# Interleaving VectorE's passes of neighbouring steps in the first block of a dense-GELU forward and backward kernel, and holding two early weight loads behind ScalarE's first activation

## The chip, the cores and the metric

The kernel runs on one core of one Trainium2 chip. The metric is the device time of one execution in microseconds; a time shown is the median of several runs. The engines are named as the profile names them: PE (TensorE), DVE (VectorE), ACT (ScalarE), POOL (GpSimd) and SP (SyncE, which here only issues transfers).

## The reference

A dense layer with GELU and a second dense layer, and the gradients of everything for a given `grad_out`. All tensors are bf16; S = 2048 rows, D = 448, F = 1792.

```python
def _fwd_reference(x, w1, b1, w2, b2):
    h = jnp.einsum("bsd,df->bsf", x, w1) + b1
    h = _gelu(h)                      # the tanh form
    return jnp.einsum("bsf,fd->bsd", h, w2) + b2

def reference(x, w1, b1, w2, b2, grad_out):
    _out, _vjp = jax.vjp(_f, x, w1, b1, w2, b2)   # _f is _fwd_reference
    _grads = _vjp(grad_out)
    return (_out, *_grads)            # out, gx, gw1, gb1, gw2, gb2
```

With u = x w1 + b1, h = gelu(u), q = grad_out w2^T and gh = q * gelu'(u), the outputs are out = h w2 + b2, gx = gh w1^T, gw1 = x^T gh, gb1 = the column sums of gh, gw2 = h^T grad_out and gb2 = the column sums of grad_out.

## The kernel before

**Tiling.** The rows are cut into four blocks of 512 (`NB`, `SB`), the hidden features into seven pairs of tiles of 128 (`NPAIR`), taken in the order `FP = [1, 2, 3, 4, 5, 6, 0]`. One *step* is one pair in one block, so there are 28 steps (`NSTEP`). Everything is held transposed, features on the partitions: for a step PE makes u (2 x 512 columns in two PSUM banks, `pu`) and q (two banks, `pq`), and ACT and DVE make h (`hT`) and gh (`ghT`) from them in SBUF. Blocks that are done feed the `o` units (out) and `x` units (gx), whose matmuls (`ps`) are put between those of u and q. After the steps come the weight gradients (lines 666 to 781), 180.7 us into the profile.

**One step on ACT and DVE.** In the first eight steps (`NSINGLE = 8`) each step is done by itself; from step 8 on two steps share an instruction. `copy_u` (L346, L348) adds the bias and brings u from PSUM to `U4`. `act_square` (L355) makes a = c u^2 and `act_gelu` (L352) makes h. `dve_cubic` makes z = (a + const) u in two passes (L359 *cubic*, L360 *cubic\*u*), and `act_tanh` (L364) takes the tanh of z in place. `dve_gate` then has four passes: L370 *slope* (a + const, times -2), L371 *slope\*h* (times h), L372 *both* (one pass over a and z together, 128x2048), L373 *gate* (z times a). `dve_gh` (L386) makes gh = (1 - z) q, reading q from PSUM. The tiles a and z of a step lie in `AZ`, which has three places, step k in place k mod 3; `U4` has two places.

**The order of the work.** It is written out by hand (`tc.manual_schedule()`): each engine runs its instructions in the order of the calls, and waits on semaphores for what it needs. In the loop over i (lines 519 to 563) PE makes u of step f = i + 2 and q of step i, with matmuls of the o and x units between them. ACT has the Tanh of step i, the two copies of u of step f, Gelu of f, then Square of f. DVE has cubic of step i + 1, the four passes of gate i, then gh i (in step 1 gate first). q has one pair of PSUM banks in these steps (`two_banks(0)`, L252), so q of step i can be started (`q_tail`, through `pe_tail_pair`) when gh of step i - 1 has read the banks. u of steps 0 and 2 to 9 has one pair of banks as well, so the u products of step f wait for the copies of step f - 1.

**The start.** SP and ACT issue the first transfers. ACT's queue has the columns 256 to 512 of w1 (`load_w1`) and their last 64 rows (`load_rest`), then the warm-up activation, which brings the table load with it, and then the columns 512 to 768 of w1 and the rest of `wt1`. ACT's sequencer issues the load of columns 512 to 768 while the table load runs, since nothing makes it wait. SP has x of the first block in two transposed halves of 256 rows (L150, L153), then w1's columns 768 to 1024 and further loads. Ten matmuls on zeros (`NWAKE`) run on PE until the data is there. Step 0's u is made in the two halves of x (`pe_u_fulls`, L239).

`behind(eng, transfer)` (L126) puts a no-op on an engine that waits until the given instruction, or the given transfer, is done. What stands behind it in the queue of that engine waits as well.

Of the kernel before, what the change touches and what calls it, by code (L numbers as in the profile page):

```python
# [19 lines left out]
def kernel(  # L20
# [15 lines left out]
    nc = tc.nc  # L36
# [88 lines left out]

    def behind(eng, transfer):  # L126
        tc.add_manual_dep(eng.nop().ins, transfer.ins.name, mybir.DependencyInfo(mybir.DependencyClass.Sync, mybir.DependencyReason.DATA),
                          reason="small loads behind those needed first")

    def load_w2(eng, t0, t1):  # L130
        return eng.dma_start(out=w2_sb[:, t0:t1, :], in_=w2[t0 * P:t1 * P, :].rearrange("(ft p) d -> p ft d", p=P))
# [20 lines left out]
    load_rest(nc.scalar, 256, 512)  # L152
    nc.sync.dma_start_transpose(out=xT[0][:, :, halves[1]], in_=wide(x2, ROW0[0] + SB // 2, SB // 2, 0))  # L153
    warm = stg.tile([P, 1], F32, name="warm", tag="warm", bufs=1)
    nc.scalar.activation(out=warm[:], in_=zero[:, 0:1], func=ACT.Gelu_apprx_tanh)
    load_w1(nc.scalar, 512, 768)
    load_rest(nc.scalar, 512, 1024)
    load_w1(nc.sync, 768, 1024)
# [46 lines left out]
    def place(first, ks):  # L205
        return AZ[:, first:first + 2 * len(ks), :]

    def part_a(ks):
        k = ks[0]
        return place(4 * (k % 3) if k < NSINGLE else SETS[k // 2 % 2] + 2 * (k % 2), ks)  # L210

    def part_z(ks):
        k = ks[0]
        return place(4 * (k % 3) + 2 if k < NSINGLE else 2 * (k % 2), ks)
# [10 lines left out]
    def rows(store, ks):  # L225
        b = ks[0] // NPAIR
        return store[b][:, 2 * (ks[0] % NPAIR):2 * (ks[-1] % NPAIR) + 2, :]
# [122 lines left out]
    def act_gelu(fs):  # L350
        for r in runs(fs):
            nc.scalar.activation(out=rows(hT, r), in_=part_u(r), func=ACT.Gelu_apprx_tanh)  # L352

    def act_square(ks):
        nc.scalar.activation(out=part_a(ks), in_=part_u(ks), func=ACT.Square, scale=math.sqrt(3.0 * GELU_A * GELU_C))  # L355

    def dve_cubic(ks):
        z = part_z(ks)
        nc.vector.tensor_scalar(out=z, in0=part_a(ks), scalar1=3.0 * GELU_C, scalar2=None, op0=ALU.add)  # L359
        nc.vector.tensor_tensor(out=z, in0=z, in1=part_u(ks), op=ALU.mult)  # L360

    def act_tanh(ks):
        z = part_z(ks)
        nc.scalar.activation(out=z, in_=z, func=ACT.Tanh, scale=-1.0 / 3.0)  # L364

    def dve_gate(ks, between=None):
        a_, z_ = part_a(ks), part_z(ks)
        if ks[0] < NSINGLE:
            both = place(4 * (ks[0] % 3), ks + ks)
            nc.vector.tensor_scalar(out=a_, in0=a_, scalar1=GELU_C, scalar2=-2.0, op0=ALU.add, op1=ALU.mult)  # L370
            nc.vector.tensor_tensor(out=a_, in0=a_, in1=rows(hT, ks), op=ALU.mult)  # L371
            nc.vector.tensor_scalar(out=both, in0=both, scalar1=1.0, scalar2=math.sqrt(0.5), op0=ALU.add, op1=ALU.mult)  # L372
            nc.vector.tensor_tensor(out=z_, in0=z_, in1=a_, op=ALU.mult)  # L373
            return
        nc.vector.tensor_scalar(out=a_, in0=a_, scalar1=GELU_C, scalar2=None, op0=ALU.add)
        for r in runs(ks):
            nc.vector.tensor_tensor(out=part_a(r), in0=part_a(r), in1=rows(hT, r), op=ALU.mult)
        nc.vector.tensor_scalar(out=a_, in0=a_, scalar1=-0.5, scalar2=None, op0=ALU.add)
        if between is not None:
            between()  # L380
        nc.vector.tensor_scalar(out=z_, in0=z_, scalar1=1.0, scalar2=None, op0=ALU.add)
        nc.vector.tensor_tensor(out=z_, in0=z_, in1=a_, op=ALU.mult)

    def dve_gh(k):
        single = k < NSINGLE
        nc.vector.scalar_tensor_tensor(out=rows(ghT, [k]), in0=part_z([k]), scalar=1.0, in1=PQ[k][:],  # L386
                                       op0=ALU.subtract if single else ALU.add, op1=ALU.mult, reverse0=single)
# [73 lines left out]
    def evictions(most=NS):  # L461
        for un in finished[:most]:
            un.evict()
        del finished[:most]
# [23 lines left out]
    copy_u(0, "av")  # L488
    act_square([0])
    act_gelu([0])  # L490
    dve_cubic([0])
    pe_u_fulls(1)
    pe_tails([1], [])
    copy_u(1, "av")
# [14 lines left out]
    side_by_side(q_of(0, 0), q_of(0, 1))  # L509
    units_side(uns[0], False, tiles(1))  # L510
    side_by_side(q_of(0, 1, True), q_of(0, 0, True))
    dve_gate([0])
    dve_cubic([1])
    dve_gh(0)
    copy_u(2, "aa")
    act_tanh([1])
    act_gelu([2])
    act_square([2])
    for i in range(1, NSINGLE):
        f = i + LEAD  # L520
        if i < 6:
            between = [(uns[1], False, tiles(i)), (uns[0], True, tiles(i)[:1]), (uns[0], True, tiles(i)[1:]), (uns[1], True, tiles(i))]
        elif i == 6:
            between = [(uns[0], True, tiles(i)), (uns[1], False, tiles(i)[:1]), (uns[1], False, tiles(i)[1:]), (uns[1], True, tiles(i))]
        else:
            between = [(uns[0], False, range(6, 10)), (uns[0], False, range(10, 12)), (uns[0], False, range(12, 14)), (uns[0], True, range(0, 6))]
        open_u(f)
        open_q(i)
        side_by_side(u_of(f, 0, True), u_of(f, 1, True))
        units_side(*between[0])  # L530
        side_by_side(u_of(f, 1), u_of(f, 0))
        units_side(*between[1])
        pe_tail_pair(f, i, 1)
        pe_tail_pair(f, i, 0)
        units_side(*between[2])
        side_by_side(q_of(i, 0), q_of(i, 1))
        units_side(*between[3])
        side_by_side(q_of(i, 1, True), q_of(i, 0, True))
        if i < 6:
            units_side(uns[0], False, tiles(i + 1))  # L540
        if i > 1:
            act_tanh([i])
        evictions(2)
        copy_u(f, "aa")
        evictions()
        act_gelu([f])
        act_square([f])
        if i == 1:
            dve_gate([i])
            dve_cubic([i + 1])  # L550
        else:
            dve_cubic([i + 1])
            dve_gate([i])
        dve_gh(i)
        if i == 6:
            open_two(1, 2)
            uns = [open_units[-2:]]
            units_side(uns[0], False, range(0, 6))
        if i == 7:
            units_side(uns[0], True, range(6, NF))  # L560
        traffic(i)
        if i >= 6:
            stores(2, f - 1)
# [20 lines left out]
    for n in range(nq):  # L584
        i = NSINGLE + n
        k = NSINGLE + 2 * n
        ks = [k, k + 1]
        fs = [k + 2, k + 3] if k + 2 < NSTEP else []
        nxt = [k + 4, k + 5] if n >= 2 and k + 4 < NSTEP else []
        if n == 0:  # L590
            dve_cubic([k + 1])
            evictions()
        act_tanh(ks)
        dve_gate(ks, evictions)
        if n <= 2:
            for f in fs:
                pe_u_fulls(f)
        if n < 2:
            pe_tails(fs, ks)
            for q in ks:  # L600
                pe_q_fulls(q)
            for f in fs:
                copy_u(f, "aa")
            for q in ks:
                dve_gh(q)
            open_one()
            pieces(28, k + 1, k - 1)
            act_square(fs)
            act_gelu(fs)
            evictions(1)  # L610
            dve_cubic(fs)
        else:
            if fs:
                pe_tails(fs[::-1], ks[::-1])
            for f in fs[::-1]:
                copy_u(f, "aa")
            pe_q_rows(ks, nxt)
            for q in ks[::-1]:
                dve_gh(q)
            if nxt:  # L620
                open_u(nxt[0])
                side_by_side(u_of(nxt[0], 0, True), u_of(nxt[0], 1, True), slice(0, 1))
                open_two(1, 2)
                uns = open_units[-2:]
                units_side(uns, False)
                side_by_side(u_of(nxt[0], 0, True), u_of(nxt[0], 1, True), slice(1, None))
                units_side(uns, True)
                side_by_side(u_of(nxt[1], 1), u_of(nxt[1], 0))
                side_by_side(u_of(nxt[0], 1), u_of(nxt[0], 0))
            elif fs:  # L630
                uns, held = two_units(order_a[2:4]), two_units(order_a[0:2])
                units_side(uns, False)
                units_side(held, False)
                pe_tails([], [k + 2, k + 3])
                units_side(uns, True)
            if fs:
                act_square(fs)
                act_gelu(fs)
                dve_cubic(fs)
        if i == 8:  # L640
            nc.gpsimd.dma_start(out=g_low[0:DL, :], in_=gT[1][DL:P, 0, :])
            g_swap[1] = g_low
        if i == 15:
            nc.gpsimd.dma_start(out=g_low[DL:P, :], in_=gT[3][0:DL, 0, :])
            g_swap[3] = g_low
        traffic(i)
        stores(3, k + 1)
# [164 lines left out]
```

## Time and profile before

| what | value |
|---|---|
| median of 3 runs | 270.99 us (270.85 to 271.34) |
| the profiled execution | 270.91 us, its span 269.1 us |
| busy: PE, DVE, ACT, POOL | 262.2, 175.8, 138.7, 40.5 us |
| PE's first product of u, first and second half of x | 5.94 and 7.21 us |
| start of step 8's work on PE | 53.2 us |
| start of the weight gradients on PE | 180.7 us |
| granted TensorE clock | full speed in the whole span |

The time of an execution is the span in the profile plus what lies around it, here 1.8 us. A line of the view in order of time has the start in us from the start of the span, the duration, the engine, the line of the kernel and the operation, out<-in, the shapes and a count; what ended the engine's idle time ahead of it stands in brackets. A line of the chain of waits has a start, a length and what the end of the kernel depended on in that stretch. A line of the view of waits has who waited for whom, the total in us, how often, and the longest. A queue's line has packets, MB, and the time that its packets took as a share of the 16 DMA engines' time; q1 is SP's queue and q10 ACT's.

### The profile page before, as it was taken

What the parts mean: (1) busy time and instruction counts of PE and PEld (TensorE: products, weight loads), DVE (VectorE), ACT (ScalarE), POOL (GpSimd) and SP (SyncE); (2) the same over time, 40 slices, a digit from 0 to 9 for tenths busy, and PEclk for the clock granted to TensorE, in tenths of its full rate; (3) what the DMA queues carried; (4) which work ended last, traced back from release to release, by engine and by line L of the source; (5) the groups of instructions that cost most, each with busy time, mean ns of one, the idle gap of its engine ahead of it and who ended that gap; (6) DMA issues with size and microseconds to landing.
All of it is one profiled execution on the core that took longest, in us unless ns stands there. A gap on an engine that the chain in (4) does not pass through costs nothing.

```text
span 269.1 us, 4993 instructions
## 1 busy us (share of the span) xinstructions
PE 262.2 (97%) x2082; PEld 157.3 (58%) x2082; DVE 175.8 (65%) x202; ACT 138.7 (52%) x162; POOL 40.5 (15%) x52
## 2 busy tenths in 40 slices
PE   6999999999999999999999999999999999999995
PEld 2358567844445665555657888874444665555554
DVE  2599999899999889687898831219999991000000
ACT  2699889799995867968668420022111211121111
POOL 1001004011002020110202030311600008900000
PEclk9999999999999999999999999999999999999999
DMA  7999999999999996172561449999411102998971
GB/s 159 249 259 190 181 154 228 171 251 211 274 232 227 253 217 156 37 189 53 152 148 47 78 86 258 357 216 263 106 40 39 51 20 50 213 227 211 163 160 34
DMA packets 111734, 44.46 MB, mean 165 GB/s; under 512 B 91040, under 2 KB 110576, under 8 KB 111712
## 3 DMA queue, kind: packets, MB, share of 16 engines
q1 hardware_dynamic: 104608, 36.14, 66.1%
q0 software_dynamic: 1856, 4.30, 5.7%
q10 hardware_dynamic: 5248, 3.71, 5.1%
q8 instruction: 16, 0.26, 0.4%
q14 instruction: 6, 0.05, 0.1%
HBM read 7.23 MB, written 14.23 MB: 80 GB/s over the span
## 4 chain that ended last, share of the span: by engine, by line
PE 85%; DVE 8%; ACT 3%; DMA 2%; SPq 0%; issue 0%; DVEq 0%; ACTq 0%
PE ps L263 27%; PE ps_v L764 16%; PE ps_w L732 14%; PE pq L263 11%; PE pu L263 9%; PE pu L242 3%; PE ps_w L743 2%; PE pq L303 2%; PE ps L416 2%; DMA xT<-in_x_dram 2%; DVE ghT L386 1%; DVE AZ L360 1%; ACT AZ L355 1%; DVE AZ L372 1%; DVE AZ L371 1%; DVE AZ L373 1%
## 5 line engine op out<-in xcount | busy, mean ns | idle before, releaser
L263 PE MATMUL ps<-w_sb,hT 64*128 64x448 bf16 x432 | 51.7, 349 | 0.3 <-ACT hT L352 0.3
L263 PE MATMUL pq<-gT,w2T 64*128 64x512 bf16 x338 | 50.0, 376 | 0.6 <-DVE ghT L386 0.4
L346 ACT ACTIVATE U<-pu,b1T 128x512 bf16<-128x512 f32 x54 | 33.3, 686 | 18.8 <-PE pu L263 18.8
L386 DVE SCALAR_TENSOR_TENSOR ghT<-AZ,pq 128x1024 bf16<-128x1024 bf16 x28 | 33.8, 1220 | 13.4 <-PE pq L263 12.1
L764 PE MATMUL ps_v<-g_nat,h_nat 128*128 128x448 bf16 (+1 forms) x240 | 42.6, 340 | 0.0
L263 PE MATMUL ps<-w1T_sb,ghT 64*128 64x448 bf16 x392 | 40.8, 349 | 0.0
L430 POOL DMA_DIRECT2D out_dram<-st x32 | 19.1, 601 | 138.8 <-ACT st L427 85.7
L263 PEld LDWEIGHTS <-hT 64*128 64x128 bf16 x432 | 28.9, 94 | 14.8 <-ACT hT L352 0.8
L732 PE MATMUL ps_w<-gh_nat,x_nat 128*128 128x512 bf16 (+1 forms) x192 | 36.5, 352 | 0.0
L764 PEld LDWEIGHTS <-h_nat 128*128 128x128 bf16 x240 | 23.3, 98 | 19.3 <-DMA out_dram<-st 0.3
L263 PEld LDWEIGHTS <-ghT 64*128 64x128 bf16 x392 | 28.6, 94 | 9.3
L263 PE MATMUL pu<-xT,w_f 64*128 64x512 bf16 x228 | 33.4, 376 | 0.0
L263 PEld LDWEIGHTS <-w2T 64*128 64x128 bf16 x344 | 25.7, 94 | 10.3 <-PE pq L263 0.4
L364 ACT ACTIVATE AZ<-AZ 128x2048 bf16<-128x2048 bf16 (+1 forms) x18 | 27.5, 1526 | 7.7 <-DVE AZ L360 7.6
L718 DVE TENSOR_TENSOR acc<-acc,gh_nat 128x1792 f32<-128x1792 f32 x14 | 30.0, 2142 | 0.5
L732 PEld LDWEIGHTS <-x_nat 128*128 128x128 bf16 x192 | 18.7, 98 | 17.9 <-issue 0.4
L355 ACT ACTIVATE AZ<-U 128x1024 bf16<-128x1024 bf16 (+1 forms) x19 | 27.6, 1454 | 0.7 <-DVE U L348 0.4
L352 ACT ACTIVATE hT<-U 128x1024 bf16<-128x1024 bf16 (+1 forms) x20 | 27.7, 1388 | 0.2
L767 ACT CAST st<-ps_v 128x448 bf16<-128x448 f32 (+1 forms) x15 | 7.6, 507 | 34.8 <-PE ps_v L764 32.3
L427 ACT CAST st<-ps 128x448 bf16<-128x448 f32 x20 | 9.8, 531 | 30.4 <-PE ps L263 29.0
L735 ACT CAST st<-ps_w 128x512 bf16<-128x512 f32 (+1 forms) x12 | 6.4, 532 | 28.0 <-PE ps_w L732 28.0
L263 PEld LDWEIGHTS <-w_f 64*128 64x128 bf16 x228 | 15.1, 94 | 8.5 <-issue 0.2
(58 smaller groups left out, 214.6 us busy)
## 6 DMA issues: line engine op xcount, KB each, us to landing
hT_dram<-hT SPq DMA_DIRECT2D x28, 256.0 KB, 3.1
out_dram<-st POOLq DMA_DIRECT2D x32, 112.0 KB, 3.8
x_nat<-in_x_dram SPq DMA_DIRECT2D x1, 1792.0 KB, 10.3
g_nat<-in_grad_out_dram SPq DMA_DIRECT2D x1, 1792.0 KB, 15.4
out_dram<-st ACTq DMA_DIRECT2D x13, 112.0 KB, 3.3
out_dram<-st ACTq DMA_DIRECT2D x9, 128.0 KB, 1.7
w_f<-in_w_dram SPq DMA_DIRECT2D x5, 192.0 KB, 4.6
w_sb<-in_w_dram SPq DMA_DIRECT2D x4, 224.0 KB, 3.9
```

The costliest lines, as they stand in the source:

```text
L242: nc.tensor.matmul(PU[f][a][:, rs], lhsT=w1_f[:, kt, cols(p, a)], rhs=xT[b][:, kt, rs], start=(kt == 0 and rs.start == 0), stop=False, ski ...
L263: mm = nc.tensor.matmul(ps, lhsT=w, rhs=m, start=start, stop=stop, tile_position=(hf.start, 0), skip_group_check=True)
L346: nc.scalar.activation(out=dst, in_=PU[f][a][:], func=ACT.Identity, bias=bias)
L352: nc.scalar.activation(out=rows(hT, r), in_=part_u(r), func=ACT.Gelu_apprx_tanh)
L355: nc.scalar.activation(out=part_a(ks), in_=part_u(ks), func=ACT.Square, scale=math.sqrt(3.0 * GELU_A * GELU_C))
L364: nc.scalar.activation(out=z, in_=z, func=ACT.Tanh, scale=-1.0 / 3.0)
L386: nc.vector.scalar_tensor_tensor(out=rows(ghT, [k]), in0=part_z([k]), scalar=1.0, in1=PQ[k][:], op0=ALU.subtract if single else ALU.add, o ...
L427: nc.scalar.copy(out=st[:, 0:D], in_=self.ps)
L430: nc.gpsimd.dma_start(out=(out2 if self.kind == "o" else gx2)[r:r + P, :], in_=st[:, 0:D])
L718: nc.vector.tensor_tensor(out=v, in0=in0, in1=gh_nat[:, b, :, j, :], op=ALU.add)
L732: nc.tensor.matmul(ps[:, 0:n * P], lhsT=x_nat[:, st_, kt * P:(kt + 1) * P], rhs=gh_nat[:, b, ft0:ft0 + n, j, :], start=(st_ == 0), stop=(s ...
L764: nc.tensor.matmul(ps[:, 0:w], lhsT=h_nat[ft][:, st_, :], rhs=g_nat[:, st_, h * w:(h + 1) * w], start=(st_ == 0), stop=(st_ == NS - 1))
```

## The change

Four things are edited.

1. DVE's passes in steps 0 to 7. They are called by name through a new function, `dve_chain`, in another order. A step has the same seven passes on the same tiles. In step i (2 to 6) the order is now both i, cubic\*u i+1, gate i, slope i+1, gh i, slope\*h i+1, cubic f. Steps 0, 1 and 7 are the run-in and the run-out of that, and cubic and cubic\*u of step 9 move into step 7.
2. ACT makes Square ahead of Gelu from step 2 on, in the loop and just before it.
3. The warm-up activation is given to `behind` on ACT, so ACT's queue waits until the activation is done before it issues the loads that stand behind it.
4. The branch of `dve_gate` for single steps goes away, since `dve_chain` has its passes.

```diff
-    nc.scalar.activation(out=warm[:], in_=zero[:, 0:1], func=ACT.Gelu_apprx_tanh)
+    behind(nc.scalar, nc.scalar.activation(out=warm[:], in_=zero[:, 0:1], func=ACT.Gelu_apprx_tanh))
     load_w1(nc.scalar, 512, 768)
     load_rest(nc.scalar, 512, 1024)
...
     def dve_gate(ks, between=None):
         a_, z_ = part_a(ks), part_z(ks)
-        if ks[0] < NSINGLE:
-            both = place(4 * (ks[0] % 3), ks + ks)
-            nc.vector.tensor_scalar(out=a_, in0=a_, scalar1=GELU_C, scalar2=-2.0, op0=ALU.add, op1=ALU.mult)
-            nc.vector.tensor_tensor(out=a_, in0=a_, in1=rows(hT, ks), op=ALU.mult)
-            nc.vector.tensor_scalar(out=both, in0=both, scalar1=1.0, scalar2=math.sqrt(0.5), op0=ALU.add, op1=ALU.mult)
-            nc.vector.tensor_tensor(out=z_, in0=z_, in1=a_, op=ALU.mult)
-            return
...
+    def dve_chain(*names):
+        for name in names:
+            op, k = name.split()
+            k = int(k)
+            a_, z_ = part_a([k]), part_z([k])
+            if op == "cubic":
+                nc.vector.tensor_scalar(out=z_, in0=a_, scalar1=3.0 * GELU_C, scalar2=None, op0=ALU.add)
+            elif op == "cubic*u":
+                nc.vector.tensor_tensor(out=z_, in0=z_, in1=part_u([k]), op=ALU.mult)
+            elif op == "slope":
+                nc.vector.tensor_scalar(out=a_, in0=a_, scalar1=GELU_C, scalar2=-2.0, op0=ALU.add, op1=ALU.mult)
+            elif op == "slope*h":
+                nc.vector.tensor_tensor(out=a_, in0=a_, in1=rows(hT, [k]), op=ALU.mult)
+            elif op == "both":
+                both = place(4 * (k % 3), [k, k])
+                nc.vector.tensor_scalar(out=both, in0=both, scalar1=1.0, scalar2=math.sqrt(0.5), op0=ALU.add, op1=ALU.mult)
+            elif op == "gate":
+                nc.vector.tensor_tensor(out=z_, in0=z_, in1=a_, op=ALU.mult)
+            else:
+                dve_gh(k)
...
-    dve_cubic([0])
+    dve_chain("cubic 0", "cubic*u 0")
...
-    dve_gate([0])
-    dve_cubic([1])
-    dve_gh(0)
+    dve_chain("slope 0", "slope*h 0", "both 0", "cubic 1", "gate 0", "cubic*u 1", "slope 1", "gh 0", "slope*h 1")
     copy_u(2, "aa")
     act_tanh([1])
+    act_square([2])
     act_gelu([2])
-    act_square([2])
...
         copy_u(f, "aa")
         evictions()
+        act_square([f])
         act_gelu([f])
-        act_square([f])
         if i == 1:
-            dve_gate([i])
-            dve_cubic([i + 1])
+            dve_chain("both 1", "cubic 2", "gate 1", "cubic*u 2", "slope 2", "gh 1", "slope*h 2", "cubic 3")
+        elif i < 7:
+            dve_chain(f"both {i}", f"cubic*u {i + 1}", f"gate {i}", f"slope {i + 1}", f"gh {i}", f"slope*h {i + 1}", f"cubic {f}")
         else:
-            dve_cubic([i + 1])
-            dve_gate([i])
-        dve_gh(i)
+            dve_chain("both 7", "cubic*u 8", "gate 7", "cubic 9", "gh 7", "cubic*u 9")
...
         if n == 0:
-            dve_cubic([k + 1])
             evictions()
```

More of the change, by code (lines that the diff above doesn't have):

```diff
@@ L127, in behind @@
         tc.add_manual_dep(eng.nop().ins, transfer.ins.name, mybir.DependencyInfo(mybir.DependencyClass.Sync, mybir.DependencyReason.DATA),
-                          reason="small loads behind those needed first")
+                          reason="loads behind what is needed first")
     def load_w2(eng, t0, t1):
```

## The prediction

> **What bounds the kernel now.** I read the page first: TensorE (PE) is the busy engine, and the rest of the page has nothing that could replace it. A step below is one index k, i or f of the code.
>
> ```profile
> span 269.1 us, 4993 instructions
> PE 262.2 (97%) x2082; PEld 157.3 (58%) x2082; DVE 175.8 (65%) x202; ACT 138.7 (52%) x162; POOL 40.5 (15%) x52
> ```
>
> PE's idle time is 6.9 us in all, so only a few us could be won without taking matmuls away, so the second view is what PE waited for:
>
> ```profile
> PE pu L242 <- DMA xT<-in_x_dram: 1.6, 2, 1.1
> PE pq L263 <- DVE ghT L386: 0.4, 2, 0.2
> ```
>
> The 0.4 us behind VectorE (DVE) is too small a figure. Matmuls overlap, so PE counts as busy for some 0.38 us after it stopped starting new ones. The third view, PE in order of time, shows starts: first a step that isn't held up (i = 2), then one that is (i = 4).
>
> ```profile
> 20.49 0.92 PE L263 MATMUL pu<-xT,w_f 64*128 64x512 bf16 x6
> ...
> 22.35 0.38 PE L263 MATMUL pu<-xT,wt 64*128 64x512 bf16 x1
> 22.46 0.38 PE L263 MATMUL pq<-gT,w2T 64*128 64x512 bf16 x1
> ...
> 29.93 0.96 PE L263 MATMUL pu<-xT,w_f 64*128 64x512 bf16 x6
> ...
> 31.79 0.38 PE L263 MATMUL pu<-xT,wt 64*128 64x512 bf16 x1
> 32.39 0.37 PE L263 MATMUL pq<-gT,w2T 64*128 64x512 bf16 x1 [0.22 <-DVE ghT L386]
> ```
>
> From the tail of u to the tail of q PE takes 0.11 us in step 2 and 0.60 in step 4. The same view has 0.52 in step 3 (26.89 to 27.41), 0.60 in step 5 (36.77 to 37.37) and 0.40 in step 6 (41.94 to 42.34), and nothing of the sort in step 7 or later. Less 0.11 each, that is 0.41 + 0.49 + 0.49 + 0.29 = 1.68 us. By the starts of the steps (20.49, 25.02, 29.93, 34.91, 39.89) an unhindered step takes 4.53 and the next three 4.91, 4.98 and 4.98: 0.38 + 0.45 + 0.45, and with step 6's 0.29 it is 1.57. I use 1.6.
>
> Why PE is held up is in the chain of waits, which runs through DVE from 23 to 37 us; this is one step of it:
>
> ```profile
> 31.11 1.22 DVE ghT L386
> 32.34 0.35 DVE AZ L359
> 32.70 0.69 DVE AZ L360
> 33.40 0.35 DVE AZ L370
> ...
> 36.09 1.23 DVE ghT L386
> 37.37 0.37 PE pq L263
> ```
>
> DVE is never idle and takes 36.09 - 31.11 = 4.98 us a step, 0.45 more than PE. The q banks are one buffer in these steps, so PE's q tail of step i waits for dve_gh(i - 1), and PE goes at DVE's pace until the longer work of steps 6 and 7 lets DVE catch up. From 42.34 on PE never waits for DVE again.
>
> **The change, part by part.**
>
> *New order on DVE.* The same seven operations a step, on the same shapes, by the rows of 25 to 40 us: 0.42 + 0.69 (cubic) + 0.42 + 0.69 (slope) + 0.69 (both) + 0.69 (gate) + 1.22 (gh) = 4.82. The old order has five places where an operation reads what the one ahead wrote; those start 0.03 to 0.11 after its end (in DVE's order of time L360 begins at 32.70 where L359 ended at 32.67; L372 at 34.57 after 34.46). Two neighbours are independent:
>
> ```profile
> 32.25 0.42 DVE L359 TENSOR_SCALAR AZ<-AZ 128x1024 bf16<-128x1024 bf16 x1
> 32.70 0.69 DVE L360 TENSOR_TENSOR AZ<-AZ,U 128x1024 bf16<-128x1024 bf16 x1
> 33.31 0.42 DVE L370 TENSOR_SCALAR AZ<-AZ 128x1024 bf16<-128x1024 bf16 x1
> ```
>
> L370 starts at 33.31 though L360 runs from 32.70 for 0.69, to 33.39; L359 starts at 32.25 though L386 runs to 32.33. So an independent neighbour starts 0.08 early. In the new order of steps 2 to 6 (both i, cubic*u i+1, gate i, slope i+1, gh i, slope*h i+1, cubic f) every input is at least two operations old. With 0.08 won at all seven the step is 4.82 - 0.56 = 4.26; with nothing won it is 4.82. I take the first: three of the new seven are kinds of neighbours seen to overlap in this trace (products followed by a one-input pass twice; and two one-input passes, L378 to L381 at 56.01 + 0.69 against 56.62), and these three alone give 4.58. DVE then needs less than PE's 4.53, and the 1.6 us go.
>
> The Trainium skill ("VectorE: DVE Perf Modes", section "The DRAIN you can't avoid") speaks against this: every VectorE operation is followed by a flush of the pipe, and eight copies took the same time with a semaphore after each as with one after the last. By that rule order would be free, DVE would stay at 4.98 and the sum would lose its 1.6 us. The starts at 33.31 and 32.25 above do not agree with it, so I go by the rows.
>
> *What is late next.* In a PE step of 4.53 counted from its first u product: the copies of u can start at about 2.5 and end at 3.75 (1.27); Square and Gelu follow to about 5.7 and the next step's Tanh to 6.65 (1.04 to 1.06 each, 0.1 overlapped). The next copies are due at 7.0, so ScalarE (ACT) has 0.35 spare; its busy time of 4.2 in a step says the same. Tanh's input, cubic*u, is ready before then, since it now stands second on DVE. DVE's both starts at 6.7, that is 2.15 in its own step; both, cubic*u, gate and slope take it to about 4.35; q's last product ends at 4.43 (24.92 against 20.49), gh runs from 4.5 to 5.7, and the next q tail is at 4.53 + 1.97 = 6.50 (22.46 against 20.49). PE has 0.8 us of cover.
>
> *Square ahead of Gelu on ACT, from f = 2.* No new work and no second table load (one in the trace). Gelu's output comes 0.95 later. Its first reader is the o product at 20.11; Gelu of step 2 ends at 18.11 before and at 19.06 then, cover 1 us. Later readers come a step after. Square comes 0.95 earlier, which the cubic at the end of DVE's step needs. Cost 0.
>
> *Earlier cubic 9 and the split around step 7.* One 0.42 operation ahead of gh 7, which waited 0.81 us for PE anyway. Cost 0.
>
> *The warm-up activation ahead of ACT's later loads.* The load of w1's columns 512 to 768 goes from an issue at 1.86 to just after 3.30 (3.10 + 0.20), 1.45 later; the load of wt behind it from 3.47 to about 3.9. ACT itself has nothing else until 8.38. The first load landed 4.4 us after its issue, so then at about 7.7; PE wants it at 8.49. wt would land at 7.9 (4.0 after issue) and is wanted at 9.90. SP's queue has no new wait; its loads share the DMA engines. What this gives back is in the DMA queues from 3.9 to 4.5 us:
>
> ```profile
> q10 hardware_dynamic: 197, 0.10, 81.1%
> q1 hardware_dynamic: 17, 0.00, 2.9%
> ```
>
> ACT's queue (q10) holds the engines while the second half of x (q1, issued from 2.12 to 3.40) hardly moves; it lands at 7.2 and PE starts on it at 7.21, after a wait of 0.46. Everything after depends on that start: copies at 8.38, the chain above, and the first products of u. From 3.7 to 5.9 q10 took 44.4% of 2.2 us, 0.98; some 0.84 of it is the moved load (384 of 448 rows). At best x comes 0.84 earlier. At worst all of it falls into the second half's own stretch, 4.5 to 6.5, where q10 took 23.5% of 2 us, 0.47, already: 0.98 - 0.47 = 0.5 later. A lower bound from another row: the transposed load of equal size issued at 8.46 landed 3.6 us after issue, against 5.1 here, which would be 1.5 earlier. I take 0.4 earlier, about the middle of -0.84 and +0.5 with a lean to the gain, because the moved load won't be on the engines much before 4.6 (the first ACT load was issued at 0.72, and from 1 to 2 us the queues moved only 8 GB/s), when part of the second half should be through.
>
> *The sum.* The profiled execution took 270.91 for a span of 269.1, 1.8 around it, and lies 0.08 under the median of 270.99. 270.91 - 1.6 - 0.4 = 268.9. No PE wait shows after 42.34, so what is won there is kept to the end unless a transfer is late: the nearest is gT of block 1, which lands at 45.2 and is wanted at 48.39, then at 46.4.
>
> **Rivals.**
> - *x doesn't come earlier.* The moved load meets the second half of x rather than the first; between 5.0 and 5.8 the queues moved only 117 GB/s, and if that comes from mixing transposed and plain loads it may come again. DVE's part stays: 270.91 - 1.6 + (0 to 0.5) = 269.3 to 269.8.
> - *Only part of the overlap.* If the four unseen kinds of neighbours (one ending in a product or in gh) win nothing and wait a little, the step stays between 4.6 and 4.82 and PE still waits 0.1 to 0.3 in four steps. 270.91 - 0.64 - 0.4 = 269.9 at 4.82.
> - *Order is free on DVE.* Step stays 4.98, only x's 0.4 is left: 270.5, or no change if x doesn't move.
> - *Slower: ACT becomes the pace.* In the new order DVE's last operation of a step, cubic f, waits for ACT's Square f, which stands behind both copies, and everything behind it on DVE waits too. If the loop copies, Square, cubic, both, cubic*u, Tanh, copies took over 4.98 a step, PE would wait longer than before. ACT's 4.2 a step must grow by 0.8 to get there. With 5.2 in five steps it is 5 x 0.22 = 1.1 more, less x's 0.4: 271.6. Against it: the schedule above has 0.35 spare in that loop.
>
> **How the numbers follow.** Forecast (both parts, x 0.1 to 0.84 earlier, 268.4 to 269.2): 0.45. x much earlier (to 1.5, 267.8): 0.07. x not earlier: 0.24. Part of the overlap: 0.10. Order free: 0.07. Slower: 0.07. About 0.2% (0.54 us) is what can be told from no change here. Faster by that: 0.45 + 0.07 + 0.24 + most of 0.10 = 0.85; within it: 0.08 (order free, and the edge of the others); slower: 0.07. The range leaves out order free, slower and the lowest cases: 268.1 to 270.1.
>
> **What the new profile will show.** DVE's operations start 0.08 before the end of the one ahead, its step follows PE at about 4.53, with a wait for q's product ahead of each gh. The intervals u tail to q tail are 0.11 in steps 3 to 6. PE's second start on x is near 6.8, and the u product of step 1 follows without a wait for w1. I am wrong if DVE's step stays above 4.6, if PE waits for ACT in steps 2 to 6, if x lands after 7.2, or if PE shows new waits after 46 us.

## The result and the profile after

The changed kernel takes 269.01 us (median of 6 executions, 268.56 to 269.56) beside 270.81 for the kernel before on the same chip (270.58 to 271.34): a ratio of 0.9933, 95% interval 0.9915 to 0.995. The prediction was 268.9, with a range of 268.1 to 270.1. The profiled execution took 268.56 with a span of 266.8, 2.3 shorter than the 269.1 of before.

The head and the chain of the page after:

```profile
span 266.8 us, 5001 instructions
PE 261.6 (98%) x2082; PEld 159.9 (60%) x2082; DVE 173.4 (65%) x202; ACT 138.7 (52%) x162; POOL 40.3 (15%) x52
PE 94%; ACT 2%; DMA 2%; DVE 0%; issue 0%; ACTq 0%
```

DVE has left the chain that sets the end. All of what PE still waits for (who waited for whom, total us, times, longest):

```profile
PE pw L188 <- DVE AZ L142: 1.2, 1, 1.2
PE pu L242 <- DMA xT<-in_x_dram: 0.4, 1, 0.4
PE ps L263 <- ACT hT L352: 0.3, 1, 0.3
```

The wait for gh is gone, and the one for x is 0.4 in place of 1.6. The first and last lines stand in the same view of before too. PE in order of time, first the start, then steps 4 and 5:

```profile
5.76 1.47 PE L242 MATMUL pu<-xT,w_f 128*128 128x256 bf16 x12 [0.39 <-DMA xT<-in_x_dram]
7.17 0.60 PE L263 MATMUL pu<-xT,wt 64*128 64x512 bf16 x2
7.70 1.47 PE L242 MATMUL pu<-xT,w_f 128*128 128x512 bf16 x6
...
28.76 0.91 PE L263 MATMUL pu<-xT,w_f 64*128 64x512 bf16 x6
...
30.63 0.38 PE L263 MATMUL pu<-xT,wt 64*128 64x512 bf16 x1
30.73 0.38 PE L263 MATMUL pq<-gT,w2T 64*128 64x512 bf16 x1
...
32.27 0.91 PE L263 MATMUL pq<-gT,w2T 64*128 64x512 bf16 x6
...
33.30 0.91 PE L263 MATMUL pu<-xT,w_f 64*128 64x512 bf16 x6
```

The twelve products of step 0 on the two halves of x now run without a break, and the next group starts at 7.70, where it started at 8.49 before: 0.79. In step 4 the tail of q follows the tail of u after 0.10 (0.60 before), and the step takes 33.30 - 28.76 = 4.54. Steps 3 to 6 give the 1.57 that they lost before. 0.79 + 1.57 = 2.36, against 2.3 between the spans.

DVE in order of time, from gh of step 3 to gh of step 4. L400 is gh, L389 slope\*h, L383 cubic, L392 both, L385 cubic\*u, L394 gate, L387 slope:

```profile
28.69 1.22 DVE L400 SCALAR_TENSOR_TENSOR ghT<-AZ,pq 128x1024 bf16<-128x1024 bf16 x1
29.83 0.68 DVE L389 TENSOR_TENSOR AZ<-AZ,hT 128x1024 bf16<-128x1024 bf16 x1
30.43 0.42 DVE L383 TENSOR_SCALAR AZ<-AZ 128x1024 bf16<-128x1024 bf16 x1
31.00 0.69 DVE L392 TENSOR_SCALAR AZ<-AZ 128x2048 bf16<-128x2048 bf16 x1 [0.15 <-ACT AZ L364]
31.61 0.69 DVE L385 TENSOR_TENSOR AZ<-AZ,U 128x1024 bf16<-128x1024 bf16 x1
32.21 0.68 DVE L394 TENSOR_TENSOR AZ<-AZ 128x1024 bf16<-128x1024 bf16 x1
32.82 0.42 DVE L387 TENSOR_SCALAR AZ<-AZ 128x1024 bf16<-128x1024 bf16 x1
33.23 1.22 DVE L400 SCALAR_TENSOR_TENSOR ghT<-AZ,pq 128x1024 bf16<-128x1024 bf16 x1
```

Add start and duration: five of the seven passes end 0.07 to 0.09 after the next one has started (28.69 + 1.22 = 29.91 against 29.83). DVE's step is 33.23 - 28.69 = 4.54, PE's pace, and DVE is held twice in it. *Both* waits 0.15 for ACT's Tanh. And gh starts only 0.01 ahead of the end of slope (32.82 + 0.42 = 33.24), 0.05 after q's last product of step 4 (32.27 + 0.91 = 33.18); that hold is too short for a bracket.

The DMA queues from 3.9 to 4.5 us (packets, MB, share of the engines' time):

```profile
q1 hardware_dynamic: 291, 0.07, 82.4%
q10 hardware_dynamic: 14, 0.00, 3.0%
```

Before it was the other way round, with 81.1% for ACT's q10. The halves of x land at 5.72 and 6.37 (5.90 and 7.17 before). The load of w1's columns 512 to 768 is issued at 3.33, lands at 7.46 and is read at 7.70.

### The profile page after: what moved, and what is told of

The parts are those of the page before. It is cut to its first block, busy times and chain, and to the rows that moved or that the text cites. A ratio compares the mean times of both kernels' runs of the same rounds, so it can differ in the third digit from the quotient of the medians.

```text
span 266.8 us, 5001 instructions
## 1 busy us (share of the span) xinstructions
PE 261.6 (98%) x2082; PEld 159.9 (60%) x2082; DVE 173.4 (65%) x202; ACT 138.7 (52%) x162; POOL 40.3 (15%) x52
## 4 chain that ended last, share of the span: by engine, by line
PE 94%; ACT 2%; DMA 2%; DVE 0%; issue 0%; ACTq 0%
PE ps L263 29%; PE ps_v L774 16%; PE ps_w L742 14%; PE pq L263 13%; PE pu L263 12%; PE pu L242 4%; PE ps_w L753 2%; PE pq L303 2%; PE ps L430 2%; DMA xT<-in_x_dram 2%; ACT AZ L355 1%; ACT hT L352 1%; DVE U L348 0%; ACT U L346 0%; ACT AZ L364 0%
## 5 line engine op out<-in xcount | busy, mean ns | idle before, releaser
L263 PE MATMUL ps<-w_sb,hT 64*128 64x448 bf16 x432 | 50.7, 349 | 0.3 <-ACT hT L352 0.3
L400 DVE SCALAR_TENSOR_TENSOR ghT<-AZ,pq 128x1024 bf16<-128x1024 bf16 x28 | 33.9, 1220 | 12.8 <-PE pq L263 11.8
L263 PEld LDWEIGHTS <-w2T 64*128 64x128 bf16 x344 | 26.3, 94 | 9.5 <-PE pq L263 0.4
```

Of the source, the lines that this page charges most:

```text
L263: mm = nc.tensor.matmul(ps, lhsT=w, rhs=m, start=start, stop=stop, tile_position=(hf.start, 0), skip_group_check=True)
```

## The experiments

The theory: parting the dependent passes shortens DVE's step by what overlaps (1.6 us), and holding ACT's loads brings the start forward (0.4 or more), each without the other. The rivals were the ones on record, above all that the order on DVE is free, that the exchange of Square and Gelu does part of the work, and that the moved load only shifts the wait to another transfer. Each run stands beside the kernel before on the same chip. The first three versions below and the first repeat of the change shared one chip (before: 270.73). The two more passes, Gelu ahead of Square, the second repeat and Gelu of step 1 first shared another (270.90). ACT's loads later still, the third repeat and the two versions with the stores held shared a third (270.75).

### The new order alone

The changed kernel without the wait on ACT:

```diff
-    behind(nc.scalar, nc.scalar.activation(out=warm[:], in_=zero[:, 0:1], func=ACT.Gelu_apprx_tanh))
+    nc.scalar.activation(out=warm[:], in_=zero[:, 0:1], func=ACT.Gelu_apprx_tanh)
```

> The new order on VectorE and Square ahead of Gelu, without the wait of the warm-up activation. Theory (the predicted sum, DVE's part): the step on DVE falls from 4.98 to what PE needs, 4.53, the starts from u tail to q tail are 0.11 in steps 3 to 6, x still lands near 7.2; about 1.6 us less than before, 0.994 of its time. Rival (order is free on DVE): step 4.98, no change. Rival (the whole gain is the earlier start): no change either.

269.26 us (269.19 to 269.51), ratio 0.9946 [0.9934, 0.9959]: 1.47 under the kernel before. The second half of x lands at 7.10 (7.17 before). Of PE's waits the one for x is still there (1.1, where it was 1.6), and there is none for DVE's gh:

```profile
PE pu L242 <- DMA xT<-in_x_dram: 1.1, 2, 0.7
```

The order brings its part without the start.

### The wait alone

The kernel before with `behind` on the warm-up activation:

```diff
-    nc.scalar.activation(out=warm[:], in_=zero[:, 0:1], func=ACT.Gelu_apprx_tanh)
+    behind(nc.scalar, nc.scalar.activation(out=warm[:], in_=zero[:, 0:1], func=ACT.Gelu_apprx_tanh))
```

> The kernel before with the warm-up activation's wait alone. Theory: the second half of x lands near 6.4 instead of 7.2, and all that follows, DVE's chain too, starts 0.8 earlier; PE still waits 1.6 us for gh. In the profile 0.8 us less than before; by the median anything from 0.2 to 0.8 less, since the runs of the changed kernel lie 1.0 us apart and those of before 0.8. Rival (the chain on DVE takes the earlier start back): same time as before.

269.77 us (269.67 to 270.32), ratio 0.9966 [0.9954, 0.9979]: 0.96 less than before, over twice the 0.4 of the prediction. PE at the start, in order of time:

```profile
5.50 1.47 PE L242 MATMUL pu<-xT,w_f 128*128 128x256 bf16 x12
6.90 0.60 PE L263 MATMUL pu<-xT,wt 64*128 64x512 bf16 x2
7.66 1.47 PE L242 MATMUL pu<-xT,w_f 128*128 128x512 bf16 x6 [0.16 <-DMA w_f<-in_w_dram]
...
16.75 0.38 PE L263 MATMUL pu<-xT,wt 64*128 64x512 bf16 x1
```

Here x came so early (second half landed at 6.06) that the moved load of w1 was late: it landed at 7.62, and PE waited 0.16. That wait cost nothing. The tail of u of step 1 starts at 16.75, 9.85 after that of step 0 (6.90); before, the two are 17.82 - 7.96 = 9.86 apart, with a wait of 0.27 for Gelu of step 1 between them that is gone here. So the 1.06 won at step 0's tail is still there at step 1's (17.82 - 16.75 = 1.07). PE's intervals for gh in steps 3 to 6 stay (0.52, 0.59, 0.60, 0.40).

### Two of five dependent pairs parted

The kernel before; in steps 2 to 7 only cubic\*u and slope change places, which parts two pairs and leaves three:

```diff
-            dve_cubic([i + 1])
-            dve_gate([i])
+            a_, z_, z2 = part_a([i]), part_z([i]), part_z([i + 1])
...
+            nc.vector.tensor_scalar(out=z2, in0=part_a([i + 1]), scalar1=3.0 * GELU_C, scalar2=None, op0=ALU.add)
+            nc.vector.tensor_scalar(out=a_, in0=a_, scalar1=GELU_C, scalar2=-2.0, op0=ALU.add, op1=ALU.mult)
+            nc.vector.tensor_tensor(out=z2, in0=z2, in1=part_u([i + 1]), op=ALU.mult)
+            nc.vector.tensor_tensor(out=a_, in0=a_, in1=rows(hT, [i]), op=ALU.mult)
...
```

> The kernel before, and in steps 2 to 7 only cubic*u and slope exchanged on DVE, so that two of the five neighbours that read the output of the one ahead are parted; Tanh's input comes about 0.3 later than before, and nothing else moves. Theory (each parted pair is worth 0.08 + 0.03 to 0.11): DVE's step falls from 4.98 to 4.7 to 4.75, PE's holdup in a step from 0.45 to about 0.2, in steps 3 to 6 together 0.8 to 1.0 us less than before. Rival (order is free, the gain of the whole change comes from Tanh's earlier input): no gain, or a loss of up to 0.3.

269.69 us (269.62 to 269.88), ratio 0.9961 [0.9949, 0.9974]. One step of DVE in order of time (L386 gh, L554 cubic, L555 slope, L556 cubic\*u, L557 slope\*h, L558 both, L559 gate):

```profile
30.60 1.22 DVE L386 SCALAR_TENSOR_TENSOR ghT<-AZ,pq 128x1024 bf16<-128x1024 bf16 x1
31.74 0.42 DVE L554 TENSOR_SCALAR AZ<-AZ 128x1024 bf16<-128x1024 bf16 x1
32.07 0.42 DVE L555 TENSOR_SCALAR AZ<-AZ 128x1024 bf16<-128x1024 bf16 x1
32.41 0.69 DVE L556 TENSOR_TENSOR AZ<-AZ,U 128x1024 bf16<-128x1024 bf16 x1
33.01 0.68 DVE L557 TENSOR_TENSOR AZ<-AZ,hT 128x1024 bf16<-128x1024 bf16 x1
33.80 0.69 DVE L558 TENSOR_SCALAR AZ<-AZ 128x2048 bf16<-128x2048 bf16 x1
34.53 0.69 DVE L559 TENSOR_TENSOR AZ<-AZ 128x1024 bf16<-128x1024 bf16 x1
35.32 1.22 DVE L386 SCALAR_TENSOR_TENSOR ghT<-AZ,pq 128x1024 bf16<-128x1024 bf16 x1
```

The four neighbours that read nothing from the pass ahead start before its end (31.74 against 31.82). The three that do read it start 0.04 to 0.11 after: 33.80 against 33.69, 34.53 against 34.49, 35.32 against 35.22. The step is 4.72, against 4.98 with five dependent pairs: 0.13 for each pair parted. PE's intervals from u tail to q tail shrink to 0.26, 0.34, 0.34 and, in step 6, 0.15 (0.11 where nothing holds PE up). Nothing but the order differs here, ACT's included, so the order is not free.

### Two more passes on DVE

The changed kernel with two extra passes of 128x1024 in each of steps 2 to 6. They write a part of `gh_nat` that is filled with its real values later.

```diff
         elif i < 7:
+            for n in range(2):
+                nc.vector.tensor_scalar(out=gh_nat[:, 3, 2 * n:2 * n + 2, :, :].rearrange("p ft j f -> p ft (j f)"), in0=gT[0][:, 0:2, :],
+                                        scalar1=2.0, scalar2=None, op0=ALU.mult)
             dve_chain(f"both {i}", f"cubic*u {i + 1}", ...)
```

> The changed kernel with two more passes on VectorE in each of steps 2 to 6, 0.42 us each, 0.08 overlapped, independent of everything (they write a place that is filled later). Theory (VectorE now has slack of 0.3 a step, and 0.8 us of cover ahead of q's tail): its step becomes 4.26 + 0.67 = 4.93, 0.40 over PE's 4.53; the cover goes in steps 2 and 3, and PE then waits about 0.2, 0.4 and 0.4 in steps 4 to 6: 0.8 to 1.2 us more than the changed kernel. Rival (VectorE still sets the pace and every us on it counts): 5 x 0.67 = 3.3 us more.

269.55 us (268.87 to 269.66), ratio 0.9946 [0.9932, 0.9959], 0.96 above the changed kernel's 268.59 on this chip. The two gh that bound one step of DVE, in order of time:

```profile
30.03 1.21 DVE L400 SCALAR_TENSOR_TENSOR ghT<-AZ,pq 128x1024 bf16<-128x1024 bf16 x1
...
32.10 0.75 DVE L564 TENSOR_SCALAR gh_nat<-gT 128x1024 bf16<-128x1024 bf16 x2
32.77 0.68 DVE L392 TENSOR_SCALAR AZ<-AZ 128x2048 bf16<-128x2048 bf16 x1
...
34.92 1.21 DVE L400 SCALAR_TENSOR_TENSOR ghT<-AZ,pq 128x1024 bf16<-128x1024 bf16 x1
```

DVE's step is 34.92 - 30.03 = 4.89, with no wait in it; less 0.67 for the extra passes (32.10 to 32.77) the seven take 4.22. That is the unhindered step which the changed kernel hides behind PE's pace. At 4.89 PE waits for q's banks again, in steps 4, 5 and 6 (u tail to q tail 0.18, 0.49 and 0.31). Between the two profiled executions, 1.03 apart at 51 us, the passes account for only 0.58; the other 0.45 was there at 8.19 against 7.74, at the start. There PE started the products of step 0 from 5.77 to 6.84 one every 0.21 us, in place of 0.11, though the second half of x had landed at 6.19; why is open. So by these profiles the passes cost less than the 0.8 to 1.2 expected, in which the medians, 0.96 apart, lie: at 4.89 DVE loses 4.89 - 4.53 = 0.36 a step, and two such steps come out of the 0.8 us of cover that the prediction gave PE.

### Gelu ahead of Square again

```diff
-    act_square([2])
     act_gelu([2])
+    act_square([2])
...
-        act_square([f])
         act_gelu([f])
+        act_square([f])
```

> The changed kernel with Gelu ahead of Square again from step 2 on. Theory (PE has 0.8 us of cover, Square comes 0.95 later but cubic f stands last on VectorE): cubic 2 in step 1 moves by some 0.5 and gh 1 with it, from 1.2 to 0.7 ahead of q's tail; no change in time, within 0.1 us of the changed kernel. Rival (Square's place is what gives DVE its pace): some of the 1.6 us comes back, DVE waits for Square ahead of cubic f in every step.

269.24 us (268.48 to 269.88, and one at 273.02; 269.05 without that one), ratio 0.9942 [0.9925, 0.9959]; the changed kernel's own there is 0.9917 [0.9904, 0.993]. The intervals overlap. The profiled execution took 268.48, with no wait of PE for gh and DVE's passes as in the changed kernel. The exchange on ACT is not what removes the wait. Whether it is worth a few tenths these runs don't settle.

### The changed kernel again, three times

> The changed kernel once more, for a second profile. Its six runs lie between 268.56 and 269.56. Theory for the spread: the load of w1's columns 512 to 768 landed at 7.46 in the profiled run, the fastest, and PE reads it at 7.70; in slower runs it lands after that, and PE waits for it at the u product of step 1. Rival: x lands later in the slower runs. Expected median 269.0, 0.993 of before.

268.25 (268.06 to 268.53), ratio 0.9906 [0.9891, 0.9922]. The order alone gave 1.47 and the wait alone 0.96 on this chip; their sum is 2.43, beside the 2.48 measured. The median is under the 269.0 that I expected. The load of w1 landed at 6.58 here and PE didn't wait for it, so this run says nothing on what makes an execution slower.

> The changed kernel once more, on the same chip as the three others, as the mark to compare them with. 268.2 to 269.0, 0.991 to 0.993 of before.

268.59 (268.28 to 268.91), ratio 0.9917 [0.9904, 0.993].

> The changed kernel again, as the mark for the three others on this chip. 268.2 to 269.0, 0.991 to 0.993 of before; gT of block 1 lands later than 45 us in its profile.

268.63 (median of 12), ratio 0.9929 [0.9906, 0.9952]. Ten of the twelve lie between 268.23 and 269.23, one took 272.79, and one 272.18: the profile is of that one, and it shows what can go wrong. Its PE in order of time, at step 7:

```profile
45.58 0.38 PE L263 MATMUL pu<-xT,wt 64*128 64x512 bf16 x1
48.00 0.39 PE L263 MATMUL pq<-gT,w2T 64*128 64x512 bf16 x1 [2.04 <-DMA gT<-in_grad_out_dram]
```

gT of block 1 landed at 47.95, and PE waited for it. In the first profile of the change it landed at 45.8, for a tail of q at 46.04: the margin is 0.2 us. gT came 2.2 later than in the first profile, for two reasons of about equal size: its issue ended at 42.96 in place of 41.80, and it landed 5.0 after that in place of 4.0. The cost is more than the wait, as the busy time by stretch shows (stretch, its length, PE, PEld, DVE, ACT, POOL busy, granted clock, DMA share, GB/s):

```profile
45.60:48.00 2.40, 0.36 (x5) 0.01 (x2) 1.80 (x3) 0.00 (x0) 0.00 (x0) 1.00 1.05 199
48.00:52.00 4.00, 4.00 (x24) 1.93 (x26) 0.43 (x1) 3.27 (x4) 0.00 (x0) 0.57 1.40 159
52.00:56.00 4.00, 3.95 (x33) 1.91 (x30) 2.76 (x4) 1.35 (x3) 0.53 (x1) 1.00 0.95 86
```

After the idle stretch the granted clock is 0.57 for 4 us, some 1.7 us of work lost on top (4 x 0.43). The q tail is 48.00 - 46.04 = 1.96 behind the first profile of the change; 1.96 + 1.7 = 3.7, and the span of 270.4 is 3.6 longer. The execution of 272.79 and the one of 273.02 in the version above have a mean granted clock of 0.993 and 0.994, like the profiled one (0.994), where the others of both versions have at least 0.998; those two weren't profiled.

### ACT's loads later still

The changed kernel with ACT's later loads held until the second half of x has landed, which asks how late that load of w1 may come:

```diff
-    nc.sync.dma_start_transpose(out=xT[0][:, :, halves[1]], ...)
+    second = nc.sync.dma_start_transpose(out=xT[0][:, :, halves[1]], ...)
...
-    behind(nc.scalar, nc.scalar.activation(out=warm[:], ...))
+    nc.scalar.activation(out=warm[:], ...)
+    behind(nc.scalar, second)
```

> The changed kernel, but ACT's loads behind the warm-up activation wait for the second half of x instead of for that activation. x is then alone with SP's loads and lands at 6.0 to 6.4 as in the changed kernel; the load of w1's columns 512 to 768 is issued at 6.1 to 6.4 rather than 3.3 and lands at 9.7 to 10.3. Theory (the wait of the change is near the point where it costs more than it gives: PE reads these columns at 7.6): PE waits 2.0 to 2.7 us at the u product of step 1 and all of it shows: near the time of before, 270.6 to 271.3. Rival (PE has room later and catches up): less than 1 us over the changed kernel.

273.86 us (272.42 to 275.5), ratio 1.0105 [1.0077, 1.0134]: slower than before. x landed at 5.43 and 5.96, no earlier than in the changed kernel on the same chip (5.36 and 5.96), and PE stood for w1. The busy time by stretch, columns as above:

```profile
7.10:10.60 3.50, 0.38 (x2) 0.00 (x0) 1.86 (x3) 2.69 (x3) 0.00 (x0) 1.00 1.22 262
10.60:13.70 3.10, 3.03 (x7) 0.83 (x8) 0.01 (x1) 0.00 (x0) 0.00 (x0) 0.52 1.08 264
```

PE's second group started at 10.67 instead of 7.70, and then ran at half the clock for 3 us. It cost more than I had expected for that second reason. The profiled execution took 272.62, with a mean clock of 0.992; the four slower ones show 0.987 to 0.988.

### Gelu of step 1 first

The changed kernel still has PE waiting 0.27 for Gelu of step 1, at 14.12. Here ACT makes that Gelu ahead of Square 1, and the run-in of DVE is put in order for it.

```diff
-    act_square([1])
     act_gelu([1])
+    act_square([1])
...
-    dve_chain("slope 0", "slope*h 0", "both 0", "cubic 1", "gate 0", "cubic*u 1", "slope 1", "gh 0", "slope*h 1")
+    dve_chain("slope 0", "slope*h 0", "both 0", "gate 0", "cubic 1", "slope 1", "cubic*u 1", "gh 0", "slope*h 1")
     copy_u(2, "aa")
-    act_tanh([1])
     act_square([2])
+    act_tanh([1])
```

> The changed kernel with Gelu 1 ahead of Square 1 and Square 2 ahead of Tanh 1 on ScalarE, and gate 0 ahead of cubic 1 on VectorE (step 0's chain: both 0, gate 0, cubic 1, slope 1, cubic*u 1, gh 0). PE's last wait of the first block, from 13.47 to 14.12 for Gelu 1 (0.65 against 0.22 without a wait), goes, since Gelu 1 would end at about 13.1. Theory (PE bounds everything behind it and the covers hold: gh 0 ends within 0.1 of q's tail, gh 1 and gh 2 0.15 ahead of theirs): 0.43 us less than the changed kernel. Rival (ScalarE, busy without a break from 8.65 to 19.2, is the true pace of the start): PE waits as long at the u products of step 2, no gain.

268.87 us (268.57 to 270.15), ratio 0.9939 [0.9919, 0.996]: not better than the changed kernel. The wait for Gelu is gone, and two others have come (PE's waits, profiled execution of 270.07):

```profile
PE pq L263 <- DMA gT<-in_grad_out_dram: 1.2, 1, 1.2
PE pu L242 <- DMA w_f<-in_w_dram: 0.5, 1, 0.5
```

gT of block 1 landed at 47.52.

### Stores held back behind gT

gT of block 1 lands later after its issue in the change than before: 4.0 us after the issue's end against 2.4. POOL's stores of `out` run at the same time, so in this version POOL waits for gT before it issues those of step 6 (`loads_g[1]` is the transfer of gT):

```diff
+        if i == 6:
+            behind(nc.gpsimd, loads_g[1])
         evictions(2)
```

> The changed kernel, and POOL's queue waits for the load of gT of block 1 before it issues the four o stores of step 6 and the two loads behind them. In the profiles of the changed kernel that load lands at 45.4 to 45.8, 4.0 after its issue ended, while the stores are issued from 40.7 on; where they are issued later it lands 2.2 to 2.4 after; PE reads it at about 46. Theory (the stores that come earlier collide with gT): gT lands at 43.2 to 44.0; the slower runs of the changed kernel, in which PE waits for gT, go; the median falls by 0.1 to 0.5 and the runs lie closer together. Rival (the spread comes from the start alone, from x or the load of w1): gT lands earlier and nothing changes in time.

268.97 us (268.6 to 269.43), ratio 0.9928 [0.9916, 0.994]. The theory fell: with the stores held until 47.08, gT was issued at 40.13 to 42.56 and landed at 46.47, still 3.9 later. The q tail started at 46.52; the view of waits blames DVE's *both* for it, which that product doesn't read.

The queues from 43 to 45.5 us in three kernels, first the one before (packets, MB, share), then the change, then this one:

```profile
q1 hardware_dynamic: 2279, 0.58, 107.3%
q0 software_dynamic: 48, 0.11, 14.4%
```

```profile
q1 hardware_dynamic: 828, 0.20, 106.7%
q0 software_dynamic: 96, 0.23, 25.1%
q8 instruction: 1, 0.02, 2.5%
```

The kernel with the stores held, over 43 to 46.5:

```profile
q1 hardware_dynamic: 2293, 0.58, 134.1%
q8 instruction: 1, 0.02, 2.0%
```

q1, which carries gT, is as occupied as before, but moves 0.20 MB in place of 0.58. In the change's stretch one packet of 16 KB of instructions appears, at 43.55, and 0.67 us later the packets of 256 bytes on q1 start to take up to 1.37 us each. Of fourteen profiles, the eight in which such a packet ran between 43.2 and 45.0 have gT 3.9 to 5.0 us after its issue; the six with the packet later (45.4 to 47.7) have it after 2.1 to 2.4. Three of those six also show packets of over 1 us on q1 within 2 us after the instructions, by when gT had landed. That is agreement in time in every profile, not proof: no run moved the fetch by itself, and what sets its time I haven't found.

### Both together

The stores held, and Gelu of step 1 first:

> The same hold of POOL's queue, with Gelu 1 ahead of Square 1, Square 2 ahead of Tanh 1 and step 0's chain as in the earlier run. There PE took all of the first block's steps without a wait for Gelu 1, but waited 1.5 us for gT at step 7 and 0.5 for the load of w1's columns 512 to 768. Theory (both waits are transfers that are late for a PE that runs ahead): with the hold the one for gT goes, and the 0.43 us of Gelu 1 shows, less what PE loses to w1 in the execution: 0.3 to 0.5 us under the run with the hold alone, 0.990 of before. Rival: gT is late for another reason (its own issue came 1.1 later there), and nothing is won.

268.57 us (268.18 to 270.68), ratio 0.9914 [0.9901, 0.9927], against 268.63 for the change on the same chip: no gain that can be told. Five of six executions lie at 268.18 to 268.94. The profiled one took 270.68, with gT at 48.12 and PE at 48.17; the issue of gT had ended at 43.92, 2.1 later than in the first profile of the change.

This profile, which has no wait for w1, bears out the rival that stood against Gelu of step 1 first, that ACT is the pace of the start. PE doesn't wait for Gelu, but its next products of u take 1.21, where they take 0.91 in the change:

```profile
14.64 1.21 PE L264 MATMUL pu<-xT,w_f 64*128 64x512 bf16 x6
```

Their banks come free with the copies of u of step 2, which ACT has from 13.75 to 15.00, and ACT works without a break from 8.43 to 26.24. The tail of u of step 1 starts 16.76 - 6.95 = 9.81 after that of step 0, where it is 9.85 in the change: 0.04 of the 0.43 that I expected is won. No version beat the change.

## Why the prediction was right, and where it wasn't

**PE was held up by DVE, and DVE by its order: right.** The order alone takes 1.47 us off, the profiles show 1.57 by the starts of the steps, and I had 1.6. DVE's share of the chain went from 8% to 0%.

**Every independent neighbour starts 0.08 early: right, the four unseen kinds too.** I had 4.26 for the step. It is hidden in the changed kernel, and 4.22 with the extra passes that bring it out. The rival of partial overlap (4.6 to 4.82) falls by that; the rival "order is free" falls by the version that parts two pairs only, where 4.98 became 4.72. The Trainium skill ("VectorE: DVE Perf Modes", section "The DRAIN you can't avoid") says that a flush follows every operation and that semaphores between operations cost nothing. The same section says that an operation which isn't held starts earlier. By these runs a neighbour that waits for the one ahead starts 0.03 to 0.11 after its end, and one that doesn't starts 0.08 ahead of it.

**What the step would look like: one wait not foreseen.** I expected a wait for q's product ahead of each gh. In step 4 gh is held by about 0.07, which fits that; a wait for q is listed only from step 6 on (0.37 at 42.67). The wait that is listed in step 4 is 0.15 for Tanh, ahead of *both*, which I hadn't named. ACT was nearer to being the pace than the 0.35 us of spare time suggested, but it wasn't the pace, and the rival of 271.6 falls: PE's step is 4.54.

**Square ahead of Gelu costs nothing: not refuted.** PE shows no new wait for h. The version with the old order on ACT can't be told from the change by its interval.

**The earlier cubic 9: 0, as said.** PE shows no wait for DVE after step 6.

**x comes earlier: right in kind, mis-sized.** This is the term that was off: 0.4, between my two ends with a lean to the gain, where the profile has 0.79 and the version with the wait alone 0.96. My upper end of 0.84 was nearly the whole truth. I had reasoned that the moved load wouldn't be on the engines much before 4.6; it took 81.1% of them from 3.9 to 4.5, a row that I had shown myself, and in the changed kernel x's queue has 82.4%. PE's second start "near 6.8" became no second start at all: the second half is there, at 6.37, before the first is used up. The rival of x not earlier falls. Its mixing of loads falls too: ACT's queue has nothing in the slow stretch after 4.5 now (88 GB/s from 4.5 to 5.0), and the stretch is still slow.

**u of step 1 without a wait for w1: right, barely.** I had the landing at about 7.7 for a use that I left at 8.49. But the use moves too, to 7.70, and the landing was at 7.46. In the version with the wait alone PE waited 0.16 for it, in the last profile of the change 0.28 (at 7.68); neither reached step 1's tail, which stands 9.85 and 9.86 after step 0's. When the start comes forward, what is wanted next is wanted sooner.

**The next late transfer: named, its margin too large.** I gave gT of block 1 from 45.2 to 46.4, 1.2 us. The use came to 46.04, but the landing also moved, to 45.8. I had taken the landing from the trace of before as if it stood still. New waits after 46 us were one of my signs of being wrong: the first profile has none, the last has one of 2.04 at 48.00.

**The sum.** The terms as measured, 270.91 - 1.57 - 0.79, give 268.55, and the profiled execution was 268.56. The median of 269.01 is 0.45 above it. That it falls within 0.1 of my 268.9 is luck: I had the start 0.39 too small, and the median execution is 0.45 slower than the profiled one. In the three later groups the change's medians are 268.25, 268.59 and 268.63. Its executions range over 1.5 us without the two above 272, those of the kernel before over 1.0. What makes a few tenths isn't shown. The profiles have two things of that size: a tail of q that stood 0.55 longer for gT (the version with the stores held), and first products one every 0.21 us, which cost 0.65 with two more passes and 0.2 and 0.08 in two profiles of the change. Of the change's 27 executions two took over 272, of the 43 of the kernel before none: the shorter margin of gT has a price, in the one that was profiled at least.

## What to carry to other kernels

On VectorE, put between two passes where the second reads the first some pass of another step, where there is one: each parted pair gave 0.13 us here, and it counts where the engine sets the pace, which shows in starts rather than in the total of waits. A load that isn't needed first can be held back by hanging it behind work that its queue has anyway; how far is set by its own first use, which moves forward with the rest, and by what else the engine waits for there (a wait of 0.28 for w1 cost nothing here). After making a stage faster, look at the margin of each transfer that it uses, and take the landing as something that moves as well.

## What I had not expected of the hardware

- A wait of PE of 2.4 us between starts cost about 1.7 us more, in a granted clock of 0.57 over the next 4 us; one of 3.6 us was followed by 0.52 over 3.1 us. Waits of 1.6 and 1.8 us, in the two versions with Gelu 1 first, were followed by a full clock. The Trainium skill ("TensorE: Matmul & The Clock Gate", section "Why this matters for your kernels") warns of gaps of over about 3 us; here 2.4 was enough once.
- After a packet of 16 KB of instructions, 256-byte packets on SP's queue took up to 1.3 to 1.5 us each, in all four profiles of the change, and gT landed 4.0 to 5.0 us after the end of its issue there, where it lands after 2.1 to 2.4 in the six profiles with a later packet. Cause open.
- The second half of x lands at 5.9 to 6.4 with ACT's loads held and at 7.1 to 7.2 without, on the same and on other chips.
